# Attention and Fourier mixer on one core: the stores of the old x, the early flag, and new orders of first loads and PSUM banks

## The chip, the cores and the metric

One NeuronCore of a Trainium2 chip. The metric is the time of one execution on the device in microseconds (us), lower is better. The kernel is already tuned: TensorE (PE below) is busy 95% of the span. ACT is ScalarE, DVE is VectorE, POOL is GpSimd, SP is SyncE, which issues most of the transfers. "Slot" means one step of the kernel's schedule: two score tiles, their exps, and the two value products of the slot before. "Phase 0" is the attention of batch 0, the first 24 slots; "phase 1" is the next 24, in which the mixer of batch 0 runs beside the attention of batch 1. The names of the tiles in the profiles: `tp` and `xt` are transposes on PE, `m` is the mask, `s` the scores, `e` the exps, `o` the value products, `sp` the row sums, `st` the first step behind the attention (it turns the sums), `hp` and `y` the two products of the channel mixer. PEld is the loading of weights into PE; "x8" after a group is the number of its instructions.

## The reference, cut to what matters

```python
# B, H, S, D = 4, 8, 768, 64; d_model = 512
scores = scale * np.matmul(q, k.transpose(0, 1, 3, 2))
# ... mask: blocks of 32: neighbours, first and last, three random ones per block
scores = np.where(mask, scores, -1e9)
attn = np.exp(scores - max); attn /= attn.sum(-1) + 1e-9
x = matmul(attn, v)                                # -> (B, S, H*D)
X = np.fft.fft(np.fft.fft(x, axis=1), axis=2)
u = x + np.real(X)
un = (u - mean) / sqrt(var + 1e-6)
out = u + np.maximum(un @ w_ch1, 0) @ w_ch2        # w_ch1 512x2048, w_ch2 2048x512
```

q, k and v are float32. The two weights lie in memory as 64-bit floats; the kernel loads them in chunks of 512 KB (`w_load`) and rounds them to float32 on ACT and DVE (`w_round`) during the attention of the first batches.

## The kernel before

The program is a hand-written order of steps, written out slot by slot by Python code that keeps an estimate of when each engine is free (`when`) and when each PSUM bank is (`free`). Small steps wait in the list `short` until `gap` finds room for them between PE's large ones. The parts that the change touches:

```python
# first loads (SyncE unless a queue is named)
load_k(0, nc.scalar)
load_q_half(0, 0)
load_v(0, nc.scalar)
load_q_half(0, 1, [nc.sync, nc.scalar])
nc.scalar.activation(out=sm.tile([P, 1], FP32, tag="nm", name="nm"), in_=neg_half, func=ACT.Exp)
...
# PSUM: "s" 2 tiles of two banks, "o" 1 bank, "t" 1 bank, "m" 2 banks
def small(batch):
    return (ps_m, "m") if batch == 0 else (ps_t, "t")

def turn(n, a, half):                 # transpose half of q (a = 0) or k (a = 1)
    ...
    pool, tag = small(pairs[max(n - 1, 0)][0])
    tp, at = pool.tile([P, 512], FP32, tag=tag, name="tp"), bank(tag)
    for c in range(T):
        nc.tensor.transpose(tp[:, c * P:(c + 1) * P], t[:, T * half + c, :, :], ident)
    nc.scalar.copy(out=dst[:, half * HS:(half + 1) * HS], in_=tp[:, 0:HS])
...
def place(n, half):                   # transpose the outputs of two heads back, copy into x
    ...
    pool, tag = small(b)
    xt, at = pool.tile([P, 512], FP32, tag=tag, name="xt"), bank(tag)
    for c in range(T):
        nc.tensor.transpose(xt[:, c * P:(c + 1) * P], oT[:, c * P:(c + 1) * P], ident)
    nc.scalar.copy(out=x_of[b, half][:, :, j * P:(j + 1) * P], in_=...)
...
def slot(sl):
    ...
    if sl > 0 and s == 3 and sl <= B * SB:
        b, j = pairs[n]
        if j == 0 and b >= 2:
            until(lambda: (b - 2, 0) in finished)     # the last rows of the old x are computed
        short.append((oT_at[n, 0], lambda: place(n, 0)))
    ...
    if s == (4 if n == 0 else 3) and n + 2 < len(pairs):
        load_q_half(n + 2, 0)
        load_q_half(n + 2, 1)
    if s == 0 and 0 < n < len(pairs) - 1:
        load_k(n + 1)
    w_loads()
...
w_load(0); w_load(1); load_k(1); load_q_half(1, 0); load_q_half(1, 1)
turn(0, 1, 0); turn(0, 0, 0)
w_loads()
for sl in range(B * SB + 1):
    slot(sl)
begin(B - 1)
for b in (B - 2, B - 1):
    until(lambda: (b, 1) in finished)
...
# flag = (largest sum of squares > LIMIT), computed here from peaks
over = nc.values_load(flag[0:1, 0:1], min_val=0, max_val=1)
with tc.If(over > 0):
    general()                                         # not taken with these data
```

x lives in two buffers per half, so batch 2 writes where batch 0 was, and must wait until batch 0's result, which is added into the same buffer, has been stored.

## Time and profile before

| | before |
|---|---|
| median of the runs beside the changed kernel | 1202.53 us (1201.79 to 1203.05, 4 runs) |
| span of the profiled run | 1198.1 us |
| PE busy, idle | 1133.0, 65.1 us |
| mean granted PE clock | 0.984 |

The profiled run was a quick one (2.7 us under the median). So a difference of two spans is some 2 or 3 us less than that of the medians. The lines themselves stand in the prediction. They are read thus: a row of the timeline gives start, duration, the group, and in brackets how long the engine was idle before it and what ended that.

### The profile page before, as it was taken

The page shows a single profiled execution, that of the slowest core. Times are in us where ns is not written, and L with a number is a line of the kernel's source. Part 1 is how long each engine was busy: PE and PEld are TensorE (multiplying, and loading weights), DVE is VectorE, ACT ScalarE, POOL GpSimd, SP SyncE. Part 2 cuts the span into 40 slices and gives each one's busy share as a digit, 9 for nine tenths or more (in the row PEclk, how much of TensorE's full clock was granted, in tenths as well). Part 3 has the DMA queues.
Part 4 walks back from the last instruction along what each step waited for, and adds up shares of the span by engine and source line. Part 5 has one row for each costly group of instructions (what it writes and reads, how often), then busy time and mean ns, then how long its engine had stood idle before and what let it go on. Part 6 is the DMA issues. An engine that isn't in the chain of part 4 may idle for free.

```text
span 1198.1 us, 11876 instructions
## 1 busy us (share of the span) xinstructions
PE 1133.0 (95%) x4412; PEld 542.6 (45%) x4412; DVE 415.6 (35%) x749; ACT 366.6 (31%) x674; POOL 247.4 (21%) x181
## 2 busy tenths in 40 slices
PE   6888988989999999799999999989999999999996
PEld 2233333434644554345444555444444554554542
DVE  4677889487103333022225553012222223000000
ACT  4676755445201321144223331034321211100100
POOL 0000057456001221033333331023331001000000
PEclk9899999989999999999999999989999999999998
DMA  4626512011001100010111010001000000001000
GB/s 135 214 83 216 174 41 67 13 35 33 1 9 27 31 1 10 18 40 14 27 31 36 14 27 2 19 20 27 1 9 18 1 1 18 9 1 27 0 9 21
DMA packets 65281, 44.26 MB, mean 37 GB/s; under 512 B 52902, under 2 KB 58048, under 8 KB 65216
## 3 DMA queue, kind: packets, MB, share of 16 engines
q1 hardware_dynamic: 62968, 42.53, 12.3%
q10 hardware_dynamic: 2248, 0.89, 0.3%
q8 instruction: 37, 0.61, 0.2%
q14 instruction: 28, 0.23, 0.1%
HBM read 37.11 MB, written 6.29 MB: 36 GB/s over the span
## 4 chain that ended last, share of the span: by engine, by line
PE 85%; DVE 4%; DMA 3%; ACT 3%; SPq 1%; issue 1%; POOL 0%; ACTq 0%; DVEq 0%; POOLq 0%
PE y L814 28%; PE hp L800 27%; PE s L471 10%; PE o L513 9%; PE tp L450 2%; PE zp L674 1%; PE zp L685 1%; DMA out_dram<-x 1%; DVE e L492 1%; DMA qr<-in_q_dram 1%; PE utp L790 1%; PE sp L561 1%; DMA wraw<-in_moe_w_ch_dram 1%; PE sp L575 1%; PE xt L532 1%
## 5 line engine op out<-in xcount | busy, mean ns | idle before, releaser
L800 PE MATMUL hp<-unT,w_sb 128*128 128x384 f32 x1024 | 342.4, 489 | 0.7 <-ACT unT L791 0.7
L814 PE MATMUL y<-w_sb,hs 128*128 128x512 f32 x768 | 337.9, 594 | 0.0
L800 PEld LDWEIGHTS hp<-unT,w_sb 128*128 128x128 f32 x1024 | 191.2, 191 | 130.7 <-issue 4.5
L501 POOL TENSOR_TENSOR acc<-acc,e 128x768 f32<-128x768 f32 x96 | 179.7, 1872 | 266.8 <-DVE e L492 262.5
L492 DVE TENSOR_TENSOR e<-s,mask 128x768 f32<-128x768 f32 x144 | 131.2, 950 | 263.0 <-ACT s L490 262.0
L814 PEld LDWEIGHTS y<-w_sb,hs 128*128 128x128 f32 x768 | 142.8, 190 | 169.8 <-issue 168.7
L471 PE MATMUL s<-qT,kT 64*128 64x384 f32 x768 | 164.2, 534 | 8.7 <-DVE e L492 6.8
L802 ACT ACTIVATE hs<-hp 128x384 f32<-128x384 f32 x128 | 62.8, 490 | 312.5 <-PE hp L800 312.5
L513 PE MATMUL o<-e,vr 128*64 128x384 f32 x768 | 147.1, 505 | 0.0
L490 ACT ACTIVATE s<-s 128x768 f32<-128x768 f32 x144 | 108.9, 793 | 93.7 <-PE s L471 92.6
L819 DVE TENSOR_TENSOR x<-y,x 128x512 f32<-128x512 f32 x24 | 16.6, 691 | 335.6 <-PE y L814 335.6
L499 POOL TENSOR_TENSOR acc<-e 128x768 f32<-128x768 f32 x24 | 45.1, 1881 | 329.3 <-DVE e L492 277.0
L471 PEld LDWEIGHTS s<-qT,kT 64*128 64x128 f32 x768 | 65.2, 191 | 76.7 <-issue 39.7
L513 PEld LDWEIGHTS o<-e,vr 128*64 128x64 f32 x768 | 47.1, 138 | 77.7 <-issue 73.6
L533 ACT COPY x<-xt 128x384 f32<-128x384 f32 x32 | 15.3, 480 | 130.1 <-DMA out_dram<-x 50.8
L450 PE MATMUL tp<-ident,qr 128*128 128x128 f32 x90 | 19.6, 317 | 22.6 <-ACT x L533 14.1
L487 ACT ACTIVATE e<-s 128x768 f32<-128x768 f32 x48 | 37.0, 802 | 3.2 <-PE s L476 3.2
L716 DVE TENSOR_TENSOR un<-pq,un 128x255 f32<-128x255 f32 x12 | 5.1, 423 | 94.7 <-ACT un L713 94.7
L749 POOL TENSOR_SCALAR rstd<-mv 128x1 f32<-128x1 f32 x24 | 6.2, 257 | 152.7 <-DVE mv L747 152.1
L791 ACT COPY unT<-utp 128x512 f32<-128x512 f32 x24 | 14.0, 585 | 72.3 <-PE utp L790 72.3
L735 DVE TENSOR_TENSOR x<-x,un 128x127 f32<-128x127 f32 x96 | 34.9, 425 | 0.1
L450 PEld LDWEIGHTS tp<-ident,qr 128*128 128x128 f32 x90 | 11.1, 148 | 38.4 <-ACT x L533 16.4
(141 smaller groups left out, 683.5 us busy)
## 6 DMA issues: line engine op xcount, KB each, us to landing
wraw<-in_moe_w_ch_dram SPq DMA_DIRECT2D x32, 512.0 KB
vr<-in_v_dram SPq DMA_DIRECT2D x30, 192.0 KB
kr<-in_k_dram SPq DMA_DIRECT2D x28, 192.0 KB
qr<-in_q_dram SPq DMA_DIRECT2D x118, 32.0 KB
out_dram<-x SPq DMA_DIRECT2D x16, 128.0 KB
out_dram<-x SPq DMA_DIRECT2D x8, 256.0 KB
qr<-in_q_dram SPq DMA_DIRECT2D x59, 31.5 KB
out_dram<-x SPq DMA_DIRECT2D x8, 126.0 KB
```

What stands on the lines that cost most here:

```text
L450: nc.tensor.transpose(tp[:, c * P:(c + 1) * P], t[:, T * half + c, :, :], ident)
L471: nc.tensor.matmul(s[:, i, 0:HS], kT[D * i:D * i + D, c * P:(c + 1) * P], qT[D * i:D * i + D, half * HS:(half + 1) * HS], start=True, stop ...
L487: nc.scalar.activation(out=e, in_=s[:, :, 0:HS], func=ACT.Exp, scale=scale)
L490: nc.scalar.activation(out=s[:, :, 0:HS], in_=s[:, :, 0:HS], func=ACT.Exp, scale=scale)
L492: nc.vector.tensor_tensor(out=e, in0=s[:, :, 0:HS], in1=m.broadcast_to([P, 2, HS]), op=ALU.mult)
L499: nc.gpsimd.tensor_add(out=acc_of[n, half], in0=e_of[u - 1], in1=e)
L501: nc.gpsimd.tensor_add(out=acc_of[n, half], in0=acc_of[n, half], in1=e)
L513: nc.tensor.matmul(o[D * i:D * i + D, :], vt[:, i, c, :], e[:, i, :], start=(c == 0), stop=(c == C - 1))
L735: tt(out=xs, in0=xs, in1=at, op=op)
L800: nc.tensor.matmul(ps[:, 0:T * P], w1_sb[:, d, f * P:(f + 1) * P], unT[half][:, d, :], start=(d == 0), stop=(d == ND - 1))
L802: nc.scalar.activation(out=hs[half, f // 4][:, f % 4, :], in_=ps[:, 0:T * P], func=ACT.Relu)
L814: nc.tensor.matmul(y, hs[half, f // 4][:, f % 4, m * P:(m + 1) * P], w2_sb[:, f, :], start=(f == 0), stop=(f == NF - 1))
```

## The change

Its intent, part by part:

1. *Stores.* The copies into a reused x are put off by 9 us (`LEAVES`) after the last row of the old x is computed, so that its store can finish under other PE work.
2. *Banks.* The transposes `tp` and `xt` always take the bank "t"; in phase 0, "m" is left to the mask and to the row sums `sp`. `gap` may now place one short step of each kind.
3. *First loads.* ACT loads its table before it issues more loads; DVE makes the first copies of q; the second half of the first q, and of the second q, are issued later.
4. *Flag.* It is computed four slots, and loaded into the engines' registers two slots, before the end of attention, and not at the end.

```diff
     load_k(0, nc.scalar)
     load_q_half(0, 0)
-    load_v(0, nc.scalar)
-    load_q_half(0, 1, [nc.sync, nc.scalar])
     nc.scalar.activation(out=sm.tile([P, 1], FP32, tag="nm", name="nm"), in_=neg_half,
                          func=ACT.Exp)
+    load_v(0, nc.scalar)
@@ turn
-        pool, tag = small(pairs[max(n - 1, 0)][0])
-        tp, at = pool.tile([P, 512], FP32, tag=tag, name="tp"), bank(tag)
+        tp, at = ps_t.tile([P, 512], FP32, tag="t", name="tp"), bank("t")
...
-        nc.scalar.copy(out=dst[:, half * HS:(half + 1) * HS], in_=tp[:, 0:HS])
-        give(at, busy("ACT", 0.5, done))
+        if n == 0 and a == 0:
+            nc.vector.tensor_copy(out=dst[:, half * HS:(half + 1) * HS], in_=tp[:, 0:HS])
+            give(at, busy("DVE", 0.55, done))
+        else:
+            nc.scalar.copy(out=dst[:, half * HS:(half + 1) * HS], in_=tp[:, 0:HS])
+            give(at, busy("ACT", 0.5, done))
@@ place
-        pool, tag = small(b)
-        xt, at = pool.tile([P, 512], FP32, tag=tag, name="xt"), bank(tag)
+        xt, at = ps_t.tile([P, 512], FP32, tag="t", name="xt"), bank("t")
@@ gap
-        if "t" not in used and min(free["t"]) <= when["PE"] + 0.1:
-            for i, (ready, fn) in enumerate(short):
-                if ready <= when["PE"] + 0.1:
-                    del short[i]
-                    fn()
-                    return
+        for item in list(short):
+            kind, ready, fn = item
+            if kind not in used and max(ready, min(free[kind])) <= when["PE"] + 0.1:
+                used += kind
+                short.remove(item)
+                fn()
@@ slot (the same for half 1, which moves from s == 2 to s == 1)
+            at = oT_at[n, 0]
             if j == 0 and b >= 2:
                 until(lambda: (b - 2, 0) in finished)
-            short.append((oT_at[n, 0], lambda: place(n, 0)))
+                at = when["PE"] + LEAVES
+            short.append(("t", at, lambda: place(n, 0)))
...
+        if sl == 0:
+            load_q_half(1, 1, [nc.sync, nc.scalar])
@@ start
     load_q_half(1, 0)
-    load_q_half(1, 1)
-    state["got"] = 2
+    w_load(2)
+    state["got"] = 3
     turn(0, 1, 0)
     turn(0, 0, 0)
-    w_loads()
+    load_q_half(0, 1, [nc.sync, nc.scalar])
     for sl in range(B * SB + 1):
         slot(sl)
+        if sl == B * SB - 4:
+            flag = highest()
+        if sl == B * SB - 2:
+            over = nc.values_load(flag[0:1, 0:1], min_val=0, max_val=1)
@@ end: the computation of the flag and its load are taken out here
```

(Cut: the kinds "t" and "m" put into every `short.append`, and the body of `highest`, which is the removed text.)

## The prediction

> **What bounds the kernel now.** I read the page first: TensorE (PE) is busy 1133.0 of 1198.1 us, and the chain that ended last is its own work.
>
> ```profile
> PE 1133.0 (95%) x4412; PEld 542.6 (45%) x4412; DVE 415.6 (35%) x749; ACT 366.6 (31%) x674; POOL 247.4 (21%) x181
> PE 85%; DVE 4%; DMA 3%; ACT 3%; SPq 1%; issue 1%; POOL 0%; ACTq 0%; DVEq 0%; POOLq 0%
> ```
>
> The change removes no matmul. So it can only win some of PE's idle 65 us, or time in which PE ran at a reduced clock. Next I cut the span into windows of 30 us and added up PE's idle time: 9.7 us in the first 30, 14.6 from 30 to 156 (the first batch, "phase 0"), about 16 from 156 to 300 (the mixer of batch 0, with VectorE busy 23 to 27 of every 30), 6.5 near 500, 6.5 near 780, and 11.5 after the last matmul. From 300 on PE is otherwise full, so a microsecond won anywhere before arrives at the end.
>
> The two holes of 6.5 stand in the list of waits and in the timeline:
>
> ```profile
> ACT x L533 <- DMA out_dram<-x: 50.8, 2, 25.4
> PE tp L450 <- ACT x L533: 14.1, 4, 6.5
> ```
>
> ```profile
> 496.85 0.69 DVE L819 TENSOR_TENSOR x<-y,x 128x512 f32<-128x512 f32 x1 [13.04 <-PE y L814]
> ...
> 505.69 0.48 ACT L533 COPY x<-xt 128x384 f32<-128x384 f32 x1 [25.42 <-DMA out_dram<-x]
> ...
> 506.22 0.98 PE L450 MATMUL tp<-ident,qr 128*128 128x128 f32 x3 [6.50 <-ACT x L533]
> ...
> 507.12 2.93 PE L471 MATMUL s<-qT,kT 64*128 64x384 f32 x8
> ```
>
> The last row of the old x is made at 497.5; its store lets go of the buffer at 505.7, 8.1 us later. ScalarE (ACT) stands at the copy into the new x, behind it the only "t" bank of PSUM, and behind that PE. After it PE is slow: eight score matmuls take 2.93 us, where they take 1.49 elsewhere. The windows say why (the column after the busy times is the granted clock):
>
> ```profile
> 504.00:506.00 2.00, 0.00 (x0) 0.00 (x0) 0.00 (x0) 0.31 (x1) 0.00 (x0) 0.50 0.07 29
> 506.00:508.00 2.00, 1.78 (x7) 1.13 (x9) 0.00 (x0) 1.33 (x4) 0.00 (x0) 0.50 0.00 0
> 508.00:510.00 2.00, 2.00 (x10) 0.62 (x6) 0.35 (x1) 1.34 (x3) 0.00 (x0) 0.50 0.00 0
> ```
>
> Phase 0's idle time is many small waits for a bank, and one large one (start, duration, group, idle time before it and what ended it):
>
> ```profile
> 34.51 0.52 PE L532 MATMUL xt<-ident,oT 128*128 128x128 f32 x3 [3.59 <-DVE sums L543]
> 43.65 0.32 PE L316 MATMUL m<-at_q,at_k 24*128 24x384 bf16 x1 [0.57 <-ACT kT L451]
> 91.03 0.52 PE L532 MATMUL xt<-ident,oT 128*128 128x128 f32 x3 [1.42 <-DVE sums L545]
> 109.79 0.52 PE L532 MATMUL xt<-ident,oT 128*128 128x128 f32 x3 [1.46 <-DVE sums L545]
> ```
>
> Here tp, xt, m and sp share the two "m" banks, and sp holds one of them for three slots; the "t" bank lies unused.
>
> The start:
>
> ```profile
> 9.40 1.28 ACT L267 ACT_TABLE_LOAD   x1 [9.40 <-DMA qr<-in_q_dram]
> 9.55 0.45 PE L450 MATMUL tp<-ident,qr 128*128 128x128 f32 x1 [1.90 <-DMA qr<-in_q_dram]
> 11.70 1.65 PE L471 MATMUL s<-qT,kT 64*128 64x384 f32 x4 [1.71 <-ACT qT L451]
> ```
>
> ACT issues loads until 9.4, loads its table, and only at 10.8 copies k, which lay ready since 6.6.
>
> **What the Trainium skill says.** "TensorE: Matmul & The Clock Gate", Part 1: the PE clock is halved after an idle window of about 3.4 us and comes back after a busy one. The trace agrees: 0.50 for about 6.8 us after both holes and for about 6.7 us after the 3.59 us wait (36 to 42.6). "Perfetto Trace Analysis", the part on DMA instructions (HWDGE): a transfer's semaphore is written only when its writes are confirmed, which can be surprisingly long towards HBM; here 8.1 us from issue to release. "PSUM — Partial Sum Buffer", Engine vs sequencer instructions: ScalarE's and VectorE's queues are strict FIFO, and matmuls complete in program order, so one blocked copy or transpose blocks all behind it; this is the hole at 500. "DMA: Bandwidth & Descriptors", Latency and other measured facts: a tensor_load costs about 600 ns; at the end of this trace 0.57 us pass from the flag to the branch.
>
> **The change part by part.**
>
> (1) Copies into x wait out the stores. In the order of the changed program the copy for batch 2's half 0 no longer follows the last y. Between them on PE stand tp (0.49), 8 matmul calls of hp (2.58), scores (1.49), values (1.44), tp (0.49), 4 of hp (1.29): 7.8 us, and xt's own 0.49. The store is free at 0.69 + 8.1 = 8.8 us. ACT waits some 0.5 us there and PE not at all. Batch 3 likewise. Won per place: the hole, 6.5, and the slow clock. At 506 that was 0.49 (tp) + 1.44 (scores) + 0.2 (values) = 2.1; at 784 it was 0.49 + 1.2 (hp 3.79 against 2.58) = 1.7. Sum 8.6 + 8.2 = 16.8; I count 16.3.
>
> (2) Banks. tp and xt go to "t", m and sp keep "m". The 3.59 vanishes: xt no longer asks for sp's bank, and the next sp needs it 3.7 us later, after scores and values. With it goes the half clock from 36 to 42.6, which cost 3.3 us. The other 11.0 us of phase 0: ten waits of 0.57 to 1.0 (m after tp, mostly), two of 1.4 for sums, two of 1.0 for oT. I keep the two for oT and four of about 0.3 where tp follows xt in the one "t" bank, so 8 go. But ACT then has in a slot 1.6 (exps) + 1.9 (weights) + 0.5 (mask) + 1.0 (copies and squares) = 5.0 us of work against 5.25 of PE's, so it becomes a near bound: I take 2 off. 6 left.
>
> (3) First loads. The table load goes ahead of the other loads, VectorE copies qT: scores can start at 9.55 + 0.45 + 0.1 + 0.55 = 10.7 in place of 11.7. But the second half of q now comes late: on the sync queue first 8 q issues until 7.2, then two weights 1.2, k 1.3, eight q 5.2, one weight 0.7, then 5 at 0.7, to 19.3, and it lands some 2.3 later (as the piece issued by 7.2 was used at 9.55): 21.6. Its transpose stood at 20.5, and would come at 19.5; it waits 2. So the start gains 1.0 and gives back 2: slot 2 begins 1.0 later than before.
>
> (2) and (3) together, counted forward from there, put the end of slot 4 at 38.6 in place of 43.9: 5.3 won; a 40% risk of a half clock after the 2 us wait takes 0.7. With the 6 of (2): 10.6 in phase 0.
>
> (4) The flag. It leaves the tail, but the tail is the last store: made at 1187.17, SyncE's end waits run at 1196.2, the end is 1198.1. The flag was done at 1187.53 and its branch lay under that. Won: 0 to 0.5. Its load now stands in mid-stream on every engine: some 0.5 on PE. Net 0.
>
> (5) Phase 1 keeps its orders on PE and VectorE almost word for word, so it is shifted; a greater backlog of VectorE at its start might take 1.
>
> Sum: 16.3 + 10.6 - 1 = 26. 1202.8 - 26 = 1177.
>
> **The rivals.** (a) The stores' wait is moved, not removed: with one "t" bank any turn behind xt would stand as before if xt came 1 or 2 us early. For: 7.8 + 0.5 against 8.8 is close. Against: the next user of "t" comes a slot later. If it held, some 2 to 4 us a place would be lost: 1181 to 1184. (b) Phase 0 is bound by ACT and VectorE, not by banks: VectorE's idle time from 43 to 138 is 23 of 95 us, ACT's waits for tp some 1.8 a slot, so there is room on the mean, but both are in order. If nothing but the first hole were won: 16.3 + 5 - 1, 1182. (c) The late half of q costs more (the loads queue behind 2 MB of weights), with a half clock after it: 3 more, 1180. (d) Everything as drawn and no new wait: 1172.
>
> **Range and chances.** Part (1) is nearly certain, and alone gives 1186.5, 1.4%. The line of 2% is at 1178.8, or 24 us. The rivals a to c lie just above it, the centre just below. I say 1177, range 1169 to 1188; faster by over 2%: 0.58, within 2%: 0.41, slower: 0.01.
>
> **What would show it.** Right: no wait of ACT's x copy for out_dram above 1 us, no 0.50 clock near 500 and 780; no xt waiting for sums and no m waiting for kT or qT in the first 156 us; scores first at about 10.7; a new wait of PE for q of about 2 us near 20; phase 1's first masked exp some 10 us earlier; a tail of 11.5 us as before. Wrong: a hole of PE behind xt after the last y, PE waiting for exps (ACT) in phase 0, or holes in phase 1 that grow by what phase 0 won.

## The result, and the profile after

The changed kernel took **1182.36 us** (median of 4 runs, 1181.96 to 1185.05), the one before 1202.53: **20.2 us less, a ratio of 0.9837** (95% interval 0.982 to 0.9855). A ratio here is the mean time of one kernel's fast runs over that of the other's in the same rounds, so it is not quite the ratio of the two medians. That is within 2%: the point lay inside the predicted range, 5.4 us slower than its centre.

The page of the changed kernel, busy times and the chain by engine. PE's share in the chain rises from 85 to 88%, and DMA's falls from 3 to 2:

```profile
PE 1134.4 (96%) x4412; PEld 542.6 (46%) x4412; DVE 413.5 (35%) x751; ACT 364.8 (31%) x672; POOL 245.7 (21%) x181
PE 88%; DVE 4%; ACT 2%; DMA 2%; issue 1%; SPq 1%; POOL 0%; ACTq 0%; DVEq 0%; POOLq 0%
```

The list of waits of the changed kernel (total us, times, longest). The copy into x waits for its transpose alone; no row has `out_dram` any more. What PE waits for most is new, exps of ACT; the longest of these three waits is 4.4 us:

```profile
ACT x L529 <- PE xt L528: 27.8, 14, 4.2
...
ACT e L484 <- DMA qk<-in_q_dram: 11.3, 1, 11.3
...
PE s L468 <- ACT e L484: 8.0, 3, 4.4
```

The timeline of the changed kernel around 494, where the hole of 6.5 us was. The last addition into the old x is followed by PE work without a gap, and ACT's copy into the new x comes 11.2 us after the addition's end, without a wait for the store:

```profile
493.62 0.69 DVE L815 TENSOR_TENSOR x<-y,x 128x512 f32<-128x512 f32 x1 [13.04 <-PE y L810]
493.74 5.33 PE L796 MATMUL hp<-unT,w_sb 128*128 128x384 f32 x16
499.00 1.24 PE L468 MATMUL s<-qT,kT 64*128 64x384 f32 x6
...
505.49 0.47 ACT L529 COPY x<-xt 128x384 f32<-128x384 f32 x1
```

Now the start. First PE, then ACT, then SP, all from the timeline of the changed kernel:

```profile
9.62 1.65 PE L468 MATMUL s<-qT,kT 64*128 64x384 f32 x4 [0.65 <-DVE qT L445]
...
24.58 0.33 PE L443 MATMUL tp<-ident,qr 128*128 128x128 f32 x1 [0.65 <-DMA qr<-in_q_dram]
29.30 1.65 PE L468 MATMUL s<-qT,kT 64*128 64x384 f32 x4 [4.39 <-ACT e L484]
```

```profile
6.77 7.60 ACTq L199 DMA_DIRECT2D qr<-in_q_dram  x5
14.42 1.51 ACT L484 ACTIVATE e<-s 128x768 f32<-128x768 f32 x2 [7.64 <-DMA qk<-in_k_dram]
...
16.92 0.21 ACT L452 ACTIVATION_READ_ACCUMULATOR kr<-kr 128x1 f32 x1
23.43 4.90 ACTq L199 DMA_DIRECT2D qk<-in_q_dram  x5
28.43 1.51 ACT L484 ACTIVATE e<-s 128x768 f32<-128x768 f32 x2 [11.30 <-DMA qk<-in_q_dram]
```

```profile
9.03 8.51 SPq L195 DMA_DIRECT2D qk<-in_q_dram  x8
17.58 0.59 SPq L402 DMA_DIRECT2D wraw<-in_moe_w_ch_dram  x1
18.23 3.66 SPq L199 DMA_DIRECT2D qr<-in_q_dram  x5
21.93 3.45 SPq L199 DMA_DIRECT2D qk<-in_q_dram  x5
```

The first scores come 2.1 us earlier than before (9.62 against 11.70), but slot 2 starts at 29.30 where before it started at 21.00. The second pair of exps reads scores, not q, yet its row names a load of q as what ended ACT's 11.3 us of idle time: it stood behind five loads in ACT's own queue. ACT was done at 17.1, began to issue them at 23.43 and needed 4.90 us. The same had happened once before: ACT's five loads from 6.77 to 14.37 stood in front of the first exps. The scores for these were there 2 us earlier than before, but the exps began at 14.42, 0.6 us later than before (13.85). (PE was also slow for longer: four score matmuls take 1.65 us up to 18.9, where before they took 0.92 from 16.07 on, though the clock column reads 1.00 there in both kernels. At the start the speed has to be read from the durations.) During the second wait PE had nothing to do, and its clock was halved (windows of the changed kernel; after the window's width: busy us of PE, its weight loads, DVE, ACT, POOL, then the granted clock, DMA share, GB/s):

```profile
28.00:30.00 2.00, 0.70 (x2) 0.51 (x4) 0.00 (x0) 1.57 (x3) 0.00 (x0) 0.50 0.92 341
```

Read from the first `hp` after 290 to the end, the stretch is 903.8 us long before (294.31 to 1198.1) and 886.0 after (294.53 to 1180.5). So the whole difference of the spans, 17.6, was won after 294, and phase 0 with its new banks won nothing in sum: that is where the prediction's 10.6 went.

### The profile page after: what moved, and what is told of

It is laid out like the page before. It is cut to its first block, busy times and chain, and to the rows that moved or that the text cites. A ratio compares the mean times of both kernels' runs of the same rounds, so it can differ in the third digit from the quotient of the medians.

```text
span 1180.5 us, 11884 instructions
## 1 busy us (share of the span) xinstructions
PE 1134.4 (96%) x4412; PEld 542.6 (46%) x4412; DVE 413.5 (35%) x751; ACT 364.8 (31%) x672; POOL 245.7 (21%) x181
## 4 chain that ended last, share of the span: by engine, by line
PE 88%; DVE 4%; ACT 2%; DMA 2%; issue 1%; SPq 1%; POOL 0%; ACTq 0%; DVEq 0%; POOLq 0%
PE hp L796 28%; PE y L810 28%; PE s L468 10%; PE o L510 9%; PE tp L443 2%; DVE e L489 2%; PE zp L670 1%; PE zp L681 1%; PE sp L557 1%; PE utp L786 1%; DMA qr<-in_q_dram 1%; PE xt L528 1%; PE s L473 1%; DMA wraw<-in_moe_w_ch_dram 1%; PE sp L571 1%
## 5 line engine op out<-in xcount | busy, mean ns | idle before, releaser
L510 PE MATMUL o<-e,vr 128*64 128x384 f32 x768 | 149.5, 511 | 0.0
L484 ACT ACTIVATE e<-s 128x768 f32<-128x768 f32 x48 | 36.6, 803 | 19.9 <-DMA qk<-in_q_dram 11.3
L448 ACT COPY qT<-tp 128x384 f32<-128x384 f32 x30 | 14.3, 478 | 65.3 <-PE tp L443 65.3
L448 ACT COPY kT<-tp 128x384 f32<-128x384 f32 x32 | 15.3, 479 | 32.7 <-PE tp L443 30.1
```

What stands on the lines that cost most here:

```text
L484: nc.scalar.activation(out=e, in_=s[:, :, 0:HS], func=ACT.Exp, scale=scale)
L510: nc.tensor.matmul(o[D * i:D * i + D, :], vt[:, i, c, :], e[:, i, :], start=(c == 0), stop=(c == C - 1))
```

## The experiments

Ten kernels ran, all with correct results. Times are medians; the kernel before took 1202.4, 1202.09 and 1203.17 in the three batches.

| kernel | us | ratio to before, 95% interval |
|---|---|---|
| e2: before, stores only | 1187.89 | 0.9872, 0.9851 to 0.9892 |
| e4: before, banks only | 1194.57 | 0.993, 0.9906 to 0.9954 |
| e5: before, first loads only | 1207.28 | 1.004, 1.0014 to 1.0065 |
| e1: after, second q on SyncE only | 1178.99 | 0.9795, 0.9767 to 0.9824 |
| e7: after, first loads as before | 1176.39 | 0.9788, 0.9765 to 0.9812 |
| e6: after, flag at the end | 1182.1 (one run) | |
| e11: after, late half of the first q early | 1183.01 | 0.9828, 0.9803 to 0.9852 |
| e13: after, DMA counters shifted | 1185.5 | 0.9852, 0.9835 to 0.9868 |
| e8: after, first loads mended | 1175.0 | 0.977, 0.9744 to 0.9797 |
| e9: e8, weights before q in each slot | 1169.69 | 0.9731, 0.9707 to 0.9754 |

### One part at a time: e2, e4, e5

Stores only:

```diff
+    LEAVES = 9.0
...
             if j == 0 and b >= 2:
                 until(lambda: (b - 2, 0) in finished)
-            short.append((oT_at[n, 0], lambda: place(n, 0)))
+                at = when["PE"] + LEAVES
+            short.append((at, lambda: place(n, 0)))
```

(and the same for half 1, with its step at s == 1)

> The kernel before with only the copies into x put off until the stores have landed. My theory: both holes of 6.5 us and the slow clock behind them go (8.6 + 8.2 = 16.8 us), nothing else moves: about 1186 us (before 1202.5). Rival: the copies' wait is only moved to the next user of the bank, and 2 to 4 us a place stay: 1190 to 1194. A second rival, that half of the whole gain of 20 us came from the banks and loads: 1192.

Measured: 1187.89, 14.5 less. The wait for the store is gone, and no wait of PE stands in its place: in its list of waits PE's first row is `s` for DVE, 7.0 us in 7 times, against 6.8 in 7 before. From the first `hp` to the end it takes 887.0 (before 903.8): 16.8 us. The medians show 2.3 less. Part of that may be the clock: in the profiled run phase 0 was 4.5 us slower than in that of before (the first `st` at 163.67 against 159.22). Of these, 2.3 us were lost by slot 5 (46.24 against 43.90), where the program is still the same: four score matmuls of slot 1 take 1.65 us and not 0.92. After that only one `xt` stands a slot earlier (the step at s == 1); the last section has the windows of a stretch with a halved clock there. The rival, a wait that only moves, is refuted.

Banks only:

```diff
-        pool, tag = small(pairs[max(n - 1, 0)][0])
-        tp, at = pool.tile([P, 512], FP32, tag=tag, name="tp"), bank(tag)
+        tp, at = ps_t.tile([P, 512], FP32, tag="t", name="tp"), bank("t")
```

(the same for `xt`, the mask's steps as kind "m", and the new loop of `gap`)

> The kernel before with only the banks dealt out anew (and one short item per kind of bank in a gap). If phase 0 was held up by banks, as I predicted: the 3.59 us wait, the half clock behind it (3.3 us) and some 6 us of small waits go, 8 to 13 us: 1190 to 1195. Rival, phase 0 or the mixer of batch 0 behind it is bound by VectorE and ScalarE, so that what PE wins it waits for later: 1199 to 1203.

Measured: 1194.57, 7.8 less; in the trace the first `st` comes at 151.06 in place of 159.22, 8.2 less. The 3.59 us for sums and the waits of the mask are gone. Two things are lost again (timeline of this kernel, PE): the one bank "t" makes the first transposes of q wait for the copy of k, so the first scores come at 12.75 in place of 11.70; and PE waits for exps at 90:

```profile
12.75 1.65 PE L470 MATMUL s<-qT,kT 64*128 64x384 f32 x4 [0.57 <-ACT qT L450]
...
90.13 1.55 PE L470 MATMUL s<-qT,kT 64*128 64x384 f32 x4 [2.32 <-ACT e L486]
```

First loads only:

```diff
-    load_v(0, nc.scalar)
-    load_q_half(0, 1, [nc.sync, nc.scalar])
     nc.scalar.activation(...)
+    load_v(0, nc.scalar)
...
     load_q_half(1, 0)
-    load_q_half(1, 1)
+    w_load(2)
     turn(0, 1, 0)
     turn(0, 0, 0)
-    w_loads()
+    load_q_half(0, 1, [nc.sync, nc.scalar])
     # and load_q_half(1, 1, [nc.sync, nc.scalar]) in slot 0, first qT copies on DVE
```

> The kernel before with only the new first loads (table load first, qT copied by VectorE, second halves of q late and partly on ScalarE's queue). From the two traces, slot 4 starts 7.0 us later in the changed kernel though the bank wait at 34 is gone there. Theory: the loads cost the start some 7 us and phase 1 gives little of it back: 1206 to 1211. Rival: the start's delay is absorbed later, as VectorE bounds the mixer of batch 0: 1201 to 1204.

Measured: 1207.28, 4.9 *more*, with an interval wholly above 1. The part that was to win a microsecond loses five. The first `st` comes at 166.25, 7.0 later than in the profiled run of before.

### What holds ACT at the start: e1, e11, e13

e1 takes the second q from ACT's queue:

```diff
-            load_q_half(1, 1, [nc.sync, nc.scalar])
+            load_q_half(1, 1)
```

> The changed kernel, with the second half of the second q loaded on the sync queue alone, so that ScalarE has no load to issue between its first and second pair of exps. Theory: ScalarE stood 11.3 us there (6.5 waiting to issue, 4.9 issuing) and PE 4.39 for it, then at half clock to 33.2: those go, 5 to 7 us earlier at slot 4, total 1176 to 1179. Rival: slot 1 waits for the late first q anyway (PE saw it at 24.6), and the sync queue's later loads are put off by 3.5 us: 1181 to 1184.

Measured: 1178.99, 3.4 less than the changed kernel, the upper edge of what the theory said (the runs, 1176.19 to 1182.04, just overlap those of the changed kernel, but the first `hp` comes 2.5 earlier in the trace). ACT does its second pair of exps at 18.10 and 20.04 in place of 28.43. PE still waits for the late half of the first q, until 25.93, and slot 2 begins right behind it (timeline of e1, PE):

```profile
26.19 1.26 PE L468 MATMUL s<-qT,kT 64*128 64x384 f32 x4
```

That is 3.1 us earlier than the 29.30 of the changed kernel, and still 5.2 later than the 21.00 before. So ACT's issues cost something, but two causes lay one over the other here: the late q and ACT's standing. The next two runs tell them apart.

Why should ACT stand in front of a load that needs nothing but an empty buffer? In the built program each of these loads also waits for one of eight counters, DMAHW0 to 7. They are dealt out in turn, so that a load waits until the last load with its counter, usually the one eight back, has landed. A listing of the changed kernel (a part; the numbers give the order within each engine):

```text
ACT 16  qk<-in_q_dram 128x1x64  waits DMAHW2      SP 24  qr<-in_q_dram 1x64       waits DMAHW2
ACT 17  qk<-in_q_dram 1x64      waits DMAHW3      SP 25  qr<-in_q_dram 128x1x64   waits DMAHW3
ACT 18  qk<-in_q_dram 126x1x64  waits DMAHW4      SP 26  qk<-in_q_dram 128x1x64   waits DMAHW4
ACT 19  qk<-in_q_dram 1x64      waits DMAHW6      SP 28  qk<-in_q_dram 126x1x64   waits DMAHW6
ACT 20  qk<-in_q_dram 128x1x64  waits DMAHW7      SP 29  qk<-in_q_dram 1x64       waits DMAHW7
```

A load counts on the counter that it waited for. So ACT's first load waits for SP's fourth load of the late half of q, and ACT's last for SP's fourth load of the second q. SP issues the former group until 21.89 and the latter until 25.38. Each ACT load thus waits for a load that SP has yet to issue at 21 to 25, and then for its landing some 2.3 us later: 23.4 to 27. That fits the 23.43 and the end at 28.33. The earlier five (6.77 to 14.37) wait in the same way: the fourth for the first chunk of the weights, the fifth for SP's first load of the second k.

e11 makes the late half of q early but leaves ACT's program as it is:

```diff
     w_load(1)
+    load_q_half(0, 1, [nc.sync, nc.scalar], 0)      # SyncE's part only
     load_k(1)
...
-    load_q_half(0, 1, [nc.sync, nc.scalar])
+    load_q_half(0, 1, [nc.sync, nc.scalar], 1)      # ACT's part only
```

> The changed kernel, but SyncE issues its five loads of the second half of the first q right after the first two weights, ahead of the second k and q. So that half should land by about 15 to 20 instead of 24.6, and TensorE need not wait for it. ScalarE's program is as in the changed kernel. Theory (ScalarE is held by the counters of earlier loads: its five loads of the second q wait for loads that SyncE still issues at 21 to 25): ScalarE issues them at about 23 to 28.5 as before, the second pair of exps starts at 28 to 29, TensorE's wait for exps only grows by what the wait for q shrinks, and the median stays within 1.5 of the changed kernel's 1182.4 (1181 to 1184). Rival (the late half of q is what costs, ScalarE's idle time follows from it): ScalarE issues at 17 and has its exps at 22 to 23, the median falls by 3 to 6 (1176.5 to 1179.5).

Measured: 1183.01, the same as the changed kernel. Timeline of this kernel, PE and then ACT:

```profile
23.22 0.60 PE L445 MATMUL tp<-ident,qr 128*128 128x128 f32 x3
28.75 1.65 PE L470 MATMUL s<-qT,kT 64*128 64x384 f32 x4 [4.92 <-ACT e L486]
```

```profile
21.95 5.83 ACTq L201 DMA_DIRECT2D qk<-in_q_dram  x5
27.88 1.51 ACT L486 ACTIVATE e<-s 128x768 f32<-128x768 f32 x2 [10.31 <-DMA qk<-in_q_dram]
```

PE no longer waits for the late half of q, and it gains nothing: it waits for exps until 28.75. In the changed kernel the late half of q, which the prediction had counted on, is hidden behind ACT's standing. It would not be free without that: e1 showed PE waiting for it until 25.93. ACT began 1 us earlier than expected (21.95, not 23), because the load that it waited for here, the last of SP's eight for the second q, was issued by 20.3.

e13 leaves ACT's instructions as they are too, but puts three loads into SP's queue ahead, which shifts the counters:

```diff
     w_load(2)
-    state["got"] = 3
+    w_load(3); w_load(4); w_load(5)                  # slot 0 would load these
+    state["got"] = 6
```

> The changed kernel, but the weights 3 to 5, which slot 0 would load, are loaded together with weight 2, ahead of the second half of the first q. ScalarE's program is the same instruction for instruction; only which of the eight DMA counters its five loads of the second q wait for has shifted: in the listing the first now waits for the seventh of SyncE's eight earlier loads of the second q (issued at about 16.5), the second and third for weights 2 and 4, the fourth for SyncE's first load of the late q half, where in the changed kernel the first waits for the fourth load of that half and the last for the fourth of the next. Theory: ScalarE begins to issue at 18 to 20 and not at 23.4, though SyncE's loads of q are later by 2 or 3, and its five issues then take longer than 4.9 in sum (they end at 25 to 28). Rival (something else holds ScalarE: its own earlier issues, or the data): it begins at 23.4 or later, as SyncE's loads do. TensorE has the late q half 2 to 3 later (27) but the exps are as late: median 1181 to 1187.

Measured: 1185.5. ACT begins 5 us *earlier*, though SP's loads of q come later, and then takes twice as long (timeline, ACT and SP):

```profile
18.47 9.78 ACTq L199 DMA_DIRECT2D qk<-in_q_dram  x5
```

```profile
19.86 7.12 SPq L199 DMA_DIRECT2D qr<-in_q_dram  x5
```

In this kernel ACT's first load waits for the seventh of eight SP loads that were all issued by 17.63, and its fourth for one issued after 19.86. It starts at 18.47 and ends at 28.25. The start follows the counter, not ACT's own earlier work and not the data. With e11 this settles it: ACT stood in its loads' waits for counters that SP's later loads held.

e7 undoes all of part 3 in the changed kernel (first loads and the first copies of q as before):

> The changed kernel with the first loads, and the copies of the first q, as they were before; banks, stores and flag stay changed. Theory: the new first loads cost, and the banks alone won 8 us and the stores alone 14.5, so this is 4 to 7 us faster than the changed kernel: 1175 to 1179. Rival: with the banks dealt out anew the loads no longer matter, since VectorE bounds the mixer of batch 0: 1181 to 1184.

Measured: 1176.39, 25.7 less than before and 6.0 less than the changed kernel. So parts 1, 2 and 4 together won as much as the prediction wanted of the whole change, and part 3 took 6.0 of it back.

### The flag: e6

```diff
-        if sl == B * SB - 4:
-            flag = highest()
-        if sl == B * SB - 2:
-            over = nc.values_load(flag[0:1, 0:1], min_val=0, max_val=1)
...
+    flag = highest()
+    over = nc.values_load(flag[0:1, 0:1], min_val=0, max_val=1)
     with tc.If(over > 0):
```

> The changed kernel with the flag made and loaded after the last y, as before. One look, for the tail: from the end of the last addition to the end of the span it was 10.9 us before and 9.9 in the changed kernel. If the flag is what lengthens the tail, 10.9 again, and about 1 us more in all; if the difference is the store's landing by chance, 9.9.

Measured: 1182.1 in one run, so no difference can be read from the time. The trace is finer. From the end of the last addition to the end of the span it is 10.93 us before (1187.17 to 1198.1), 10.84 here (1169.56 to 1180.4), and 11.03, 11.09 and 11.28 in e2, e4 and e5, all with the flag at the end. With the early flag it is 9.86 in the changed kernel (1170.64 to 1180.5), and 9.88 to 9.94 in e1, e7, e8, e9, e11 and e13. The early flag is worth 1.0 us, five kernels against seven. The source view of the branch line has ACT's semaphore event at 1177.1 in e6, 3.3 us before the end, and at 1131.4 in the changed kernel, far ahead of it. That ACT's late arrival is what holds the end is argued from this, not isolated. In mid-stream the flag cost PE nothing that shows: after 300 no wait of PE stands in the changed kernel's trace.

### A better order: e8, e9

e8 keeps the new table load and the first copies on DVE, but issues the late half of q early, and the second q on SyncE alone:

```diff
                          func=ACT.Exp)
+    load_q_half(0, 1, [nc.sync, nc.scalar])
     load_v(0, nc.scalar)
...
-    load_q_half(0, 1, [nc.sync, nc.scalar])          # after the first turns
-            load_q_half(1, 1, [nc.sync, nc.scalar])  # in slot 0
+    load_q_half(1, 1)                                # after w_load(2)
```

> The changed kernel with the table load still first and VectorE still copying the first q, but the second half of the first q issued at once after the first half (both queues, ahead of v), and the second half of the second q on the sync queue right after the third weight, so that ScalarE issues nothing once the exps have begun. Theory: no wait for q near 23, no wait for exps near 29, slot 4 near 31 in place of 42: 1171 to 1176. Rival: ScalarE's seven issues ahead of the copy of k hold that copy until 10 to 11 us, as in the kernel before: like e7, 1176 to 1179.

Measured: 1175.0, in the expected range, but not for the reason given: slot 4 began at 35.16 and not at 31. The copy of k again came behind seven issues of ACT (4.25 to 9.35), so the first scores came at 11.48. The times of e7 and e8 can't be told apart, and so part 3, even mended, is not shown to win anything.

e9 adds one line's move, aimed at the wait for exps at 90 to 98:

```diff
+        w_loads()
         if s == (4 if n == 0 else 3) and n + 2 < len(pairs):
             load_q_half(n + 2, 0)
             load_q_half(n + 2, 1)
         if s == 0 and 0 < n < len(pairs) - 1:
             load_k(n + 1)
-        w_loads()
```

> As the mended first loads, and in every slot the weights' loads stand ahead of the q loads on the sync queue. In the changed kernel PE stood 2.9 us at 95 for exps that waited on ScalarE for a weight whose load had queued behind 18 q issues (79.3 to 90.3), and ran at half clock until 105. Theory: that wait and the half clock go, 3 to 5 us under the mended kernel: 1167 to 1172. Rival: the sync queue waits there for VectorE to free a room anyway, and the wait moves: no change.

The wait, in the timeline of the changed kernel (ACT, SP and PE in order of time): the weights stand behind 18 loads of q on SP; ACT waits for them to round them, its exps stand behind that, and PE behind the exps:

```profile
79.28 4.90 SPq L195 DMA_DIRECT2D qr<-in_q_dram  x8
84.22 6.03 SPq L199 DMA_DIRECT2D qr<-in_q_dram  x10
90.36 1.63 SPq L402 DMA_DIRECT2D wraw<-in_moe_w_ch_dram  x3
...
94.98 0.66 ACT L411 ACTIVATE wraw<-wraw 128x512 f32<-128x512 uint32 x1 [4.31 <-DMA wraw<-in_moe_w_ch_dram]
...
98.22 1.65 PE L468 MATMUL s<-qT,kT 64*128 64x384 f32 x4 [2.88 <-ACT e L484]
```

Windows of 90 to 120 us, the changed kernel, then e8, from which e9 differs by this one move, then e9:

```profile
90.00:120.00 30.00, 27.12 (x149) 9.22 (x147) 21.33 (x48) 20.14 (x36) 0.00 (x0) 0.89 0.66 214
```

```profile
90.00:120.00 30.00, 27.84 (x156) 9.52 (x157) 24.52 (x58) 22.85 (x41) 0.00 (x0) 0.89 0.52 164
```

```profile
90.00:120.00 30.00, 29.03 (x185) 10.21 (x184) 26.04 (x60) 23.38 (x41) 0.00 (x0) 1.00 0.71 224
```

PE does 185 matmuls in the window in place of 149 and 156, at full clock. Measured: **1169.69, a ratio of 0.9731 to before**, 5.3 less than e8 and the best of all kernels here: 2.7% under the kernel before and 12.7 us under the changed one.

## Why the prediction was right and where it was wrong

The time lies in the predicted range, 5.4 us above its centre. It does so because step 1 came as predicted and the range reached up to little more than step 1 alone; of the 10.6 us that steps 2 and 3 were to win in phase 0, nothing is left in the sum. "Faster by over 2%", given 0.58, did not come. Rival (b) names 1182 too, but that is luck: it sets 5 us for phase 0, where in fact the banks won 7.8 and the first loads, of which it says nothing, took 6.0 back. One of the prediction's own signs of being wrong did appear, PE waiting for exps in phase 0 (4.39 and 2.88 us).

**Step 1, the stores: right.** 16.3 was predicted. Between the first `hp` and the end e2 shows 16.8, its median 14.5. In the changed kernel PE has no wait there, and its clock stays at 1.00 in the windows around 493 and 770. One reading was loose: the half clock did not last 6.8 us after the holes of the kernel before. It began inside them (0.50 from 504 and from 780 on) and lasted some 4 and 3 us after them; the cost was taken from the matmuls' durations and is not touched by that.

**Step 2, the banks: right in mechanism, too large.** The sum of the step was 3.59 + 3.3 + 6 = 12.9. Alone it is worth 7.8 by the medians and 8.2 in the trace. The named waits and their half clock did go. The term of 6 was what failed: it set 2 us aside for ACT as a near bound, but not the 1.05 us later start that the single bank "t" brings, nor the wait of 2.32 for exps with its half clock. The rival that ACT is the bound was half right: it is ACT, but it waits for a late weight load, as e9 shows by moving that load; it isn't saturated.

**Step 3, the first loads: this step failed.** "So the start gains 1.0 and gives back 2: slot 2 begins 1.0 later than before" was the claim. The first scores did come 2.1 earlier (9.62), yet slot 2 began 8.3 later (29.30 against 21.00), and the end of slot 4, put at 38.6, came at 47.2 (43.9 before). Instead of the 1.0 lost the part cost 4.9 alone and 6.0 in the changed kernel (against e7). Two terms were wrong. The late half of q was put at 21.6 and was used at 24.58, because SP's eight issues took 8.51 us and not the 5.2 of my sum. The term missing altogether was ACT: five loads stand before its first pair of exps, and the five of the second q between its first and second pair, and in the program each of these waits for the landing of an earlier load, those of the second q for SP loads that were still to come. My sum counts SP's issues alone, by what they take; ACT's are not in it, and I never asked what a load waits for. The two waits lie one over the other: taking away the late q alone wins nothing (e11), taking ACT's loads of the second q away alone wins 3.4 (e1), and with both gone 6.0 to 7.4 are won (e7, e8). So rival (c), a costlier late q, was half right: with ACT out of the way (e1) the late q still put slot 2 5.2 us later than before.

**Step 4, the flag: sized wrongly.** Net 0 was predicted; it wins 1.0 at the end and costs PE nothing visible. The argument that the tail is only the last store overlooked what else ends late there.

**Step 5, phase 1 shifted: right, within some 1 us.** What phase 0 won came through to the first `hp` (287.14 in e4, 287.30 in e7, 282.12 in e9, against 294.31 before). The 1 us set aside for a greater backlog of DVE was lost in e4 (8.2 won at the first `st`, 7.2 at the first `hp`), but not in e7 and e9 (5.8 and 10.7 at `st`, 7.0 and 12.2 at `hp`). The reading that VectorE is busy 23 to 27 of every 30 us there passes over the window from 210 to 240, with 13.0.

The single parts, with the flag's share from the tail, add up to 14.5 + 7.8 - 4.9 + 1.0 = 18.4, against 20.2 measured. They are not quite independent: banks and flag together give 11.5 on top of the stores (e2 to e7), 8.8 as single parts. Some 2 us of this stay open; the runs of one kernel scatter by as much.

## What to carry to other kernels

A load issued from a compute engine is an instruction in that engine's queue and can wait there, for an earlier load of *another* queue; before moving one between two pieces of time-critical work, list what it waits for in the built program, not only what it takes to issue. If a row of compute names as its releaser a load whose data it doesn't read, look at the loads ahead of it in the same queue. And test the parts of a change singly: here one of four parts took back nearly a quarter of what the other three won, which the sum hid.

## What the Trainium skill lacked or had wrong

- "DMA: Bandwidth & Descriptors", Issuing engines are not separate DMA queues, says that initiating transfers from several engines only saves the sequencer's time, "which is usually small". Here it was no saving but a cost: ACT stood 6.3 us (17.1 to 23.43) before five small loads and 4.90 in them, and the same loads issued on SP made the kernel 3.4 us faster (e1). The same page says, in its anatomy of one DMA, that waits happen on the issuing sequencer and not in the DMA engines, and this agrees with the trace; what it lacks is that loads which share a few counters couple the queues, so that a load on ACT waits for the landing of one on SP (in e13 the start moved from 23.43 to 18.47 with nothing but the counters shifted for ACT).
- "TensorE: Matmul & The Clock Gate", Part 1, gives at least one idle window of about 3.4 us as what halves the clock, and says that the windows run freely; its part on a second failure mode tells of a kernel whose frequent short stops switched the clock to and fro, but gives no length for them. In e2, two gaps of 0.57 us with three transposes between were followed by a halved clock from 64 to about 67.5, where the kernel before, with the same two gaps around the same steps a slot later (up to 65.8 and 67.1), kept 1.00. So gaps far shorter than the window can be followed by a halved clock, and need not be; what decides it is not shown. Windows of e2 (the clock is the third number from the end):

```profile
62.00:64.00 2.00, 1.10 (x6) 0.65 (x8) 1.51 (x3) 0.79 (x3) 0.00 (x0) 1.00 0.91 308
64.00:66.00 2.00, 2.00 (x8) 0.60 (x10) 0.42 (x1) 1.72 (x4) 0.00 (x0) 0.53 0.91 292
```

- "Advanced Engine Details and Errata", Control Flow Timing, gives about 108 ns for a compare-and-branch. The flag's branch took 50 to 72 ns on ACT, DVE and SP, but 4082 ns on PE at the end (e6) and 3391 ns early (the changed kernel). No page gives a time of this size for a branch, or the cost of a flag that comes at the very end: 1.0 us of the tail here.
